# Sign transfers ahead of the q and k loads, the last pair's scaling in the gated block, and weight preparation over two pieces

## The chip, the cores and the metric

The kernel runs on one core of a Trainium2 chip, alone. The metric is the device time in microseconds of one execution of the whole program: the attention block, and the gated feed-forward block that takes its output. Five engines work side by side, each through its own list of instructions in order: TensorE (PE, with PEld for its weight loads), VectorE (DVE), ScalarE (ACT), GpSimd (POOL) and SyncE (SP). In this kernel POOL and SP do little but issue DMAs.

## What is computed

```python
# q, k, v: 4 batches x 8 heads x 768 x 64; proj: 64 x 6
q_bits = (np.einsum('bhsd,dk->bhsk', q, proj) > 0)
k_bits = (np.einsum('bhsd,dk->bhsk', k, proj) > 0)
# the buckets are the bits read as a number
mask = q_bucket[:, :, :, None] == k_bucket[:, :, None, :]
scores = np.where(mask, scale * np.matmul(q, k.transpose(0, 1, 3, 2)), -1e9)
attn = softmax(scores)
attn_out = np.matmul(attn, v)
# bridge: x is 3072 tokens x 512
g = x @ w_gate                      # 512 x 1536
silu = g * (1.0 / (1.0 + np.exp(-g)))
out = silu * (x @ w_val) @ w_out    # 1536 x 512
```

The three weight matrices are float64 and come to the chip as pairs of 32-bit words.

## The kernel before

**Attention** goes over 16 pairs of heads (4 batches of 4 pairs), each in two halves of 384 queries, each half in six chunks of 128 keys. For a chunk, PE multiplies q and k (`sc`, L427, with `T`), adds a product of bit rows (`qb`, `kb`) in the same PSUM bank, by which unequal buckets come out far below equal ones, ScalarE takes the exponential into one of eight tiles `A` (L430), and VectorE adds the tiles up into `acc` (L455, L459). After the six chunks PE multiplies them with v (`av`, L441).

The bits of pair n+1 are made in pair n's second half: PE's hash products, four sign instructions on ScalarE (L359), and for q a transfer on SP that copies the signs of 32 rows to a second place, `spread_q` (L371, qb<-qb). The first chunk of pair n+1 needs it. The q and k loads of pair n+2 (L245, and L253 from pair 5 on, eight DMAs of 96 KB) are issued on SP at the end of pair n's first half. Each has one buffer, so a load waits until pair n+1's transposes have read it: PE's transposes for the first pairs, VectorE's (L395) from pair 5 on.

The sums of pair n are made in pair n+1's first half: `total` (L464) with PE, a copy of a `row` on ScalarE (L473) and a small DMA few<-row on SP (L475). `invert` follows at the end of that half: VectorE's reciprocal (L479), then sums<-few and two r<-sums on SP (L481, L485). `norm` follows at the end of the second half: xT is scaled on VectorE (L491), and stored in DRAM (L496), or split into three parts for batch 0. For the last pair all three come after the loop (L545 to L548).

**Weight preparation** runs beside attention and the first part of the gated block. `prepare` (L131) is a generator: each piece of 128 x 512 weights takes five steps on VectorE (L140, L142, L145, L149, L151), with two scaling instructions on ScalarE ahead of them (L122, L123) and a rounding between the third and the fourth (L146). A step at the end writes the piece's three parts to DRAM from POOL (L153, ram<-stage), and later a ring tile loads them back (`bring`, L179, ring<-ram). There are 36 pieces. `prepare_on(n)` takes n steps: 4 or 5 at the end of each half in attention, one after each atom in the gated block. `scale_ahead` (L126) issues the two scaling instructions of a piece before its steps, in attention before and after the v products. Word tiles (`wordp`) have four buffers, staging tiles (`stagep`) two, ring tiles seven.

**The gated block** goes over 48 up blocks (4 batches of 12) and a down block for every three. An up block has four atoms: `one` and `other` for the gate and for the value. `one` is 16 matmuls into `a`, which ScalarE copies (L612); `other` is 8 matmuls into `n`, which VectorE subtracts (L618). The silu (L620), the product (L622), the hid copy (L623) and VectorE's two parts of it (L626, L628) follow. A down block has six atoms of nine matmuls (`o`), the first of a batch copied by ScalarE (L657). The PSUM tiles of this block are four, of two banks each, and go round: a gate's `a` and `n`, then a value's.

The order on each engine is that in which the program issues the instructions; no scheduler moves them.

Of the kernel before, what the change touches and what calls it, by code (L numbers as in the profile page):

```python
# [19 lines left out]
def kernel(  # L20
# [104 lines left out]

    def scale_ahead():  # L126
        i = progress["scaled"]
        if i < NPIECE and i < progress["kept"] + 2 and i in words:
            scale(i)

    def prepare():  # L131
        for i in range(NPIECE):
            load_words(i + 1)
            if i not in staged:
                scale(i)
            t, st = words[i], staged[i]
            lo, hi = t[:, :, 0], t[:, :, 1]
            w = st[:, 1]
            wi = w.bitcast(I32)
            nc.vector.tensor_single_scalar(wi, wi, 3, op=ALU.logical_shift_left)  # L140
            yield True
            nc.vector.scalar_tensor_tensor(out=wi, in0=hi, scalar=-(1 << 31), in1=wi,  # L142
                                           op0=ALU.bitwise_and, op1=ALU.bitwise_or)
            yield True
            nc.vector.tensor_tensor(wi, wi, lo, op=ALU.add)  # L145
            nc.scalar.activation(r32(st[:, 0]), w, AF.Copy, scale=TOWARD)  # L146
            load_words(i + 4)
            yield True
            nc.vector.tensor_tensor(r32(w), w, st[:, 0], op=ALU.subtract)  # L149
            yield True  # L150
            nc.vector.scalar_tensor_tensor(out=r32(st[:, 2]), in0=w, scalar=-STEP, in1=st[:, 0],  # L151
                                           op0=ALU.mult, op1=ALU.add)
            nc.gpsimd.dma_start(ram[i].bitcast(FP32), st)  # L153
            progress["kept"] = i + 1
            yield True
# [57 lines left out]
    def attention(scope):  # L213
# [116 lines left out]
        load_words(4)  # L330
# [79 lines left out]
        xT = {}  # L410
        mean = {}
# [21 lines left out]
        def attend(u):  # L433
# [30 lines left out]
        def total(n):  # L464
# [9 lines left out]
            few = att.tile([P, each], FP32, tag="few", name="few")  # L474
# [3 lines left out]
        def invert(n, few):  # L478
# [3 lines left out]
            t = att.tile([P, 2, HQ], FP32, tag="r", name="r")  # L482
# [72 lines left out]
    def gated_block(scope):  # L555
        xs = [even_x, scope.enter_context(tc.tile_pool(name="odd_x", bufs=1))]
# [121 lines left out]
        splits = []  # L678
        for kind, n in order:
            if kind == "U":  # L680
                b, f = divmod(n, NF)
                if f == NF - NQ and b + 1 < B:
                    for pr in range(NP):
# [3 lines left out]
                        splits += split(x, b + 1, pr, xs[(b + 1) % 2])  # L687
            if kind == "D" and n == B * NF // NQ - 1:
                finish(tails)
            for atom in atoms_of(kind, n):  # L690
# [4 lines left out]
                if splits:  # L695
                    splits.pop(0)()
                prepare_on(1)

    bring(7)
# [34 lines left out]
```

## Time and profile before

| | us |
|---|---|
| median of 8 runs | 1032.61 |
| lowest and highest | 1030.24, 1036.11 |
| the profiled execution | 1033.42 |
| its span, first to last instruction | 1031.6 |
| its mean granted PE clock | 0.965 |

Attention takes the first 418 us of the span, the gated block the rest. In the rows below, a time in front of an engine is the start from the beginning of the span, the next number is how long it took; in brackets stands for how long the engine had been idle before it, and what ended that. L numbers are lines of this kernel. In a row of a group, the numbers after the bar are the busy time in all, the mean of one in ns, and the idle time just before, with what ended it. PEclk is the clock that PE was granted, as a share of full speed. A row of a DMA with KB has the median from issue to landing as its last number.

### The profile page before, as it was taken

Reading aid. Unit: us, or ns where it says so; the run is one execution under the profiler, and the core shown is the slowest. Engines: PE = TensorE matmul, PEld = TensorE weight load, DVE = VectorE, ACT = ScalarE, POOL = GpSimd, SP = SyncE. Lnnn points to the kernel's source line nnn. Section 1 sums busy time; section 2 is a strip of 40 time slices with the busy share of each in tenths; the row PEclk is TensorE's granted clock in tenths of the full one; section 3 lists DMA queues with packets and bytes.
Section 4 is the critical chain, followed back from the end, with each engine's and each line's share of the span. In section 5 each row is a group of like instructions: output and inputs, shape, how many; then the busy total and the mean of one; then the engine's idle time right before and its main releaser. Section 6 shows DMA issues by size and latency. Waiting matters only on the chain.

```text
span 1031.6 us, 14465 instructions
## 1 busy us (share of the span) xinstructions
PE 964.8 (94%) x5413; PEld 728.4 (71%) x5413; DVE 674.3 (65%) x868; ACT 474.1 (46%) x882; POOL 125.2 (12%) x248
## 2 busy tenths in 40 slices
PE   8988888889788899599999999999999999999998
PEld 4444433334233344499999999999999999999997
DVE  5766776667567678287877654677554686555566
ACT  7877765666566668155342133232233133233221
POOL 3110000000001101132111111111101111111110
PEclk9989988889889899989999999999999999999999
DMA  7554555665656645797895575456656536746541
GB/s 200 165 156 146 134 139 128 181 181 131 181 131 181 181 130 182 276 334 265 337 341 195 192 299 198 179 174 216 247 209 245 184 135 249 259 151 217 197 171 62
DMA packets 134262, 203.22 MB, mean 197 GB/s; under 512 B 92912, under 2 KB 98512, under 8 KB 134192
## 3 DMA queue, kind: packets, MB, share of 16 engines
q0 software_dynamic: 31008, 159.79, 43.3%
q1 hardware_dynamic: 102384, 42.30, 16.2%
q8 instruction: 43, 0.70, 0.3%
q10 hardware_dynamic: 800, 0.20, 0.1%
q14 instruction: 27, 0.22, 0.1%
HBM read 162.01 MB, written 39.42 MB: 195 GB/s over the span
## 4 chain that ended last, share of the span: by engine, by line
PE 56%; DMA 2%; DVE 1%; issue 0%; SPq 0%; DVEq 0%
PE a L570 25%; PE o L570 18%; PE n L570 13%; DMA few<-row 1%; DVE o L662 0%; DVE o L659 0%; DMA r<-sums 0%; DMA sums<-few 0%; DVE g L618 0%; DVE stage L151 0%; SPq L485 0%; DVE few L479 0%; DVE xT L491 0%; DVEq L618 0%; DVEq L142 0%
## 5 line engine op out<-in xcount | busy, mean ns | idle before, releaser
L570 PE MATMUL a<-xparts,ring 128*128 128x384 f32 x1536 | 283.8, 336 | 1.9 <-ACT row L473 1.9
L570 PEld LDWEIGHTS a<-xparts,ring 128*128 128x128 f32 x1536 | 269.9, 189 | 3.8 <-ACT row L473 2.6
L570 PE MATMUL o<-ring,hid 128*128 128x512 f32 x864 | 199.1, 390 | 0.0
L427 PE MATMUL sc<-qT,kT 64*128 64x384 f32 x768 | 182.2, 539 | 13.2 <-ACT A L430 13.2
L570 PEld LDWEIGHTS o<-ring,hid 128*128 128x128 f32 x864 | 161.9, 188 | 33.1
L430 ACT ACTIVATE A<-sc 128x384 f32<-128x384 f32 x384 | 157.9, 501 | 42.6 <-PE sc L427 42.1
L427 PEld LDWEIGHTS sc<-qT,kT 64*128 64x128 f32 x768 | 79.0, 199 | 121.2 <-issue 87.6
L570 PE MATMUL n<-xparts,ring 128*128 128x384 f32 x768 | 149.9, 336 | 9.2 <-DVE g L618 9.2
L459 DVE TENSOR_TENSOR acc<-acc,A 128x768 f32<-128x768 f32 x128 | 122.7, 958 | 38.2 <-ACT A L430 27.2
L570 PEld LDWEIGHTS n<-xparts,ring 128*128 128x128 f32 x768 | 135.5, 189 | 9.5 <-DVE g L618 9.5
L441 PE MATMUL av<-A,vraw 128*64 128x386 f32 (+1 forms) x768 | 131.2, 491 | 0.0
L189 POOL DMA_DIRECT2D ring<-ram x144 | 76.1, 531 | 433.0 <-PE n L570 276.6
L618 DVE TENSOR_TENSOR v<-v,n 128x768 f32<-128x768 f32 x48 | 45.8, 954 | 105.9 <-PE n L570 104.8
L427 PE MATMUL sc<-qb,kb 64*128 64x384 bf16 x384 | 81.0, 342 | 35.5 <-DMA qb<-qb 34.9
L441 PEld LDWEIGHTS av<-A,vraw 128*64 128x64 f32 x768 | 52.3, 136 | 72.3 <-issue 60.0
L612 ACT ACTIVATE g<-a 128x768 f32<-128x768 f32 x48 | 39.0, 811 | 126.8 <-PE a L570 123.6
L623 ACT ACTIVATE hid<-v 128x768 fp32r<-128x768 f32 x48 | 40.7, 847 | 118.7 <-DVE v L622 118.7
L620 ACT ACTIVATE g<-g 128x768 f32<-128x768 f32 x48 | 40.6, 846 | 104.6 <-DVE g L618 104.6
L662 DVE TENSOR_TENSOR o<-o 128x512 f32<-128x512 f32 x96 | 65.9, 687 | 21.5 <-ACT o L657 19.0
L153 POOL DMA_DIRECT2D ram<-stage x36 | 19.7, 547 | 435.2 <-issue 228.6
L455 DVE SCALAR_TENSOR_TENSOR acc<-A 128x768 f32<-128x768 f32 x32 | 30.6, 957 | 63.5 <-ACT A L430 63.3
L618 DVE TENSOR_TENSOR g<-g,n 128x768 f32<-128x768 f32 x48 | 45.6, 950 | 30.1 <-PE n L570 30.1
(75 smaller groups left out, 732.0 us busy)
## 6 DMA issues: line engine op xcount, KB each, us to landing
ring<-ram POOLq DMA_DIRECT2D x144, 768.0 KB, 5.4
ram<-stage POOLq DMA_DIRECT2D x36, 768.0 KB, 4.9
vraw<-in_v_dram SPq DMA_DIRECT2D x16, 384.0 KB
r<-sums SPq DMA_DIRECT2D x32, 192.0 KB
words<-in_moe_w_out_dram POOLq DMA_DIRECT2D x12, 512.0 KB, 6.6
out_dram<-o SPq DMA_DIRECT2D x24, 256.0 KB
words<-in_moe_w_gate_dram POOLq DMA_DIRECT2D x11, 512.0 KB, 7.4
words<-in_moe_w_val_dram POOLq DMA_DIRECT2D x11, 512.0 KB, 7.8
```

What stands on the lines that cost most here:

```text
L189: nc.gpsimd.dma_start(t.bitcast(FP32), ram[at].bitcast(FP32))
L427: nc.tensor.matmul(sc[h], x["k", n][rows, ks], x["q", n][rows, qs], start=start, stop=not start)
L430: nc.scalar.activation(weights(u)[:, h, 0:HQ], sc[h], AF.Exp, scale=SCALE * (OFF / 2 if n <= NP else 1.0))
L441: nc.tensor.matmul(ps[h * D : (h + 1) * D, 0:width], raws["v", n][:, h, c, :], a[:, h, 0:width], start=c == 0, stop=c == NCH - 1)
L455: nc.vector.scalar_tensor_tensor(out=acc[n, half], in0=weights(u - 1)[:, :, 0:HQ], scalar=S * EPS / P, in1=a[:, :, 0:HQ], op0=ALU.add, op1 ...
L459: nc.vector.tensor_tensor(acc[n, half], acc[n, half], a[:, :, 0:HQ], op=ALU.add)
L570: nc.tensor.matmul(ps, w, x, start=start, stop=stop)
L612: nc.scalar.activation(two(z), ops[what][2], AF.Copy, scale=STEP + 1)
L618: nc.vector.tensor_tensor(two(z), two(z), n_, op=ALU.subtract)
L620: nc.scalar.activation(z, z, AF.Silu)
L623: nc.scalar.activation(h, val, AF.Copy, scale=TOWARD / STEP)
L662: nc.vector.tensor_tensor(accs[c], accs[c], t[:, 1], op=ALU.subtract)
```

## The change

There are three parts.

1. The q and k loads of pair n+2 are issued in the third chunk of pair n's second half, right behind the step that makes the signs and issues their spread, instead of at the end of the first half.
2. The last pair's `invert` and `norm` run in the gated block, after its 6th and 14th atom. Its xT and its spread reciprocals get a place in a tile of the gated block's x parts (`lastx`), so that attention's tiles can be given back. The first seven ring loads are issued one at the end of each of the last seven halves, instead of all seven behind the loop.
3. A piece's last two steps are taken after the next piece's first three, so that two pieces are under way. The rounding is no longer issued with the third step, but by the next `scale_ahead` (or at the latest ahead of the fourth step). `scale_ahead` may go three pieces beyond what is finished instead of two, and is also called after each atom of the gated block. Staging tiles get a third buffer, word tiles go from four buffers to three, and words are loaded three pieces ahead instead of four.

```diff
-    wordp = ctx.enter_context(tc.tile_pool(name="wordp", bufs=4))
-    stagep = ctx.enter_context(tc.tile_pool(name="stagep", bufs=2))
+    wordp = ctx.enter_context(tc.tile_pool(name="wordp", bufs=3))
+    stagep = ctx.enter_context(tc.tile_pool(name="stagep", bufs=3))
+    small = ctx.enter_context(tc.tile_pool(name="small", bufs=2))
+    odd_x = {NP - 1: ctx.enter_context(tc.tile_pool(name="odd_x", bufs=1))}
...
+    unrounded = []
+
+    def round_up():
+        st = staged[unrounded.pop(0)]
+        nc.scalar.activation(r32(st[:, 0]), st[:, 1], AF.Copy, scale=TOWARD)
+
     def scale_ahead():
+        if unrounded:
+            round_up()
         i = progress["scaled"]
-        if i < NPIECE and i < progress["kept"] + 2 and i in words:
+        if i < NPIECE and i < progress["kept"] + 3 and i in words:
             scale(i)
 
     def prepare():
...
+        for i in range(NPIECE + 1):
+            if i < NPIECE:
...
+                nc.vector.tensor_tensor(wi, wi, lo, op=ALU.add)
+                unrounded.append(i)
+                load_words(i + 3)
+                yield True
+            if i > 0:
+                while i - 1 in unrounded:
+                    round_up()
+                st = staged[i - 1]
+                w = st[:, 1]
+                nc.vector.tensor_tensor(r32(w), w, st[:, 0], op=ALU.subtract)
+                yield True
+                nc.vector.scalar_tensor_tensor(out=r32(st[:, 2]), in0=w, scalar=-STEP,
+                                               in1=st[:, 0], op0=ALU.mult, op1=ALU.add)
+                nc.gpsimd.dma_start(ram[i - 1].bitcast(FP32), st)
+                progress["kept"] = i
+                yield True
...
-                    xT[n] = xp.tile([P, S], FP32, tag="xT", name="xT")
-                    mean[n] = att.tile([P, 1], FP32, tag="e", name="e")
+                    if n == len(pairs) - 1:
+                        t = odd_x[NP - 1].tile([P, 3, S], FP32, tag=f"x{NP - 1}", name="lastx")
+                        xT[n], spread[n] = t[:, 0], t[:, 1]
+                    else:
+                        xT[n] = xp.tile([P, S], FP32, tag="xT", name="xT")
+                    mean[n] = small.tile([P, 1], FP32, tag="e", name="e")
...
                 if u + c == 2 or more and half == 1 and c == 2:
                     prepare_pair(1)
+                if half == 1 and c == 2:
+                    load(n + 2, "qk")
...
                 if n + 1 <= NP:
                     prepare_pair(2 if u else 4)
-                load(n + 2, "qk")
             prepare_on(5 if 0 < n < NP else 4)
+            if u >= N - 7 * NCH:
+                bring()
         total(len(pairs) - 1)
-        while waiting:
-            last.append(waiting.pop(0)())
-        finish(last)
+        left.extend(waiting)
...
+                    while next(preparing, None):
+                        pass
...
+                count[0] += 1
+                if left and count[0] in (6, 14):
+                    left.append(left.pop(0)())
+                    left[:] = [f for f in left if f]
                 prepare_on(1)
-
-    bring(7)
+                scale_ahead()
```

What moves stands in the orders of the engines. First SP, in a pair from which on each load of q or k is four DMAs; few, sums and r are the small transfers of the pair before, qb<-qb spreads the signs. Before (L253 loads q and k, L371 spreads):

```order
L475 DMA few<-row 128x1x12
L481 DMA sums<-few 128x12
L485 DMA r<-sums 64x768 x2
L253 DMA qraw<-in_q_dram 32x24x32 x4
L253 DMA kraw<-in_k_dram 32x24x32 x4
L371 DMA qb<-qb 32x768
L232 DMA vraw<-in_v_dram 128x2x384
```

And now (L268 loads, L386 spreads):

```order
L495 DMA few<-row 128x1x12
L501 DMA sums<-few 128x12
L508 DMA r<-sums 64x768 x2
L386 DMA qb<-qb 32x768
L268 DMA qraw<-in_q_dram 32x24x32 x4
L268 DMA kraw<-in_k_dram 32x24x32 x4
L247 DMA vraw<-in_v_dram 128x2x384
```

The eight loads have gone behind the spread; nothing else on SP has moved there.

Next ScalarE from the end of an early pair's second half (its signs of k are L359 before, L374 now) to the next pair's exponentials; L146 before and L132 now are the rounding, L122 and L123, now L124 and L125, the scaling. Before:

```order
L359 ACTIVATE kb<-hps,columns 32x384 x4
L200 ACTIVATE xparts<-xT 128x768
L122 ACTIVATE stage<-words 128x512
L123 ACTIVATE words<-words 128x512
L448 COPY xT<-av 128x384
L146 ACTIVATE stage<-stage 128x512
L430 ACTIVATE A<-sc 128x384 x4
```

And now:

```order
L374 ACTIVATE kb<-hps,columns 32x384 x4
L215 ACTIVATE xparts<-xT 128x768
L132 ACTIVATE stage<-stage 128x512
L124 ACTIVATE stage<-words 128x512
L125 ACTIVATE words<-words 128x512
L468 COPY xT<-av 128x384
L446 ACTIVATE A<-sc 128x384 x4
```

The rounding has gone from right ahead of the exponentials to ahead of the scaling, and it is that of the steps taken one half earlier.

Last ScalarE at the start of the gated block, now, with the buffers' numbers, from the first value's copy (L639) and hid (L650) to the second block's gate; L647 is the silu:

```order
L639 ACTIVATE v_3601<-a_3642 128x768
L650 ACTIVATE hid_3599<-v_3601 128x768
L124 ACTIVATE stage_3677<-words_3639 128x512
L125 ACTIVATE words_3639<-words_3639 128x512
L639 ACTIVATE g_3681<-a_3683 128x768
L647 ACTIVATE g_3681<-g_3681 128x768
```

And POOL at that place, where L168 writes a staging tile, L204 loads a ring tile and L117 loads words:

```order
L204 DMA ring_3670<-ram_88 128x1536
L168 DMA ram_106<-stage_3459 128x1536
L204 DMA ring_3713<-ram_89 128x1536
L117 DMA words_3742<-in_moe_w_val_dram 128x4x256
L204 DMA ring_3753<-ram_90 128x1536
L168 DMA ram_107<-stage_3542 128x1536
```

The staging tiles come in the order 3459, 3542, 3623, 3677, and there are three buffers: the tile that L124 writes here takes the buffer of 3459, which the second row of POOL's list writes out. Before, the scaling stood with the first step of its own piece, five steps after the write that it waits for. The gate copy of the second block (g_3681) stands behind the scaling.

More of the change, by code (lines that the diff above doesn't have):

```diff
@@ L410, in attention @@
         xT = {}
+        spread = {}
         mean = {}
@@ L473, in total @@
             nc.scalar.copy(row, ps[:, 0:HQ])
-            few = att.tile([P, each], FP32, tag="few", name="few")
+            few = small.tile([P, each], FP32, tag="few", name="few")
             nc.sync.dma_start(few, row.rearrange("(g r) t -> r g t", r=BLOCK)[0])
@@ L481, in invert @@
             nc.sync.dma_start(s, few)
-            t = att.tile([P, 2, HQ], FP32, tag="r", name="r")
+            if n == len(pairs) - 1:
+                t = spread[n].rearrange("p (x q) -> p x q", x=2)
+            else:
+                t = att.tile([P, 2, HQ], FP32, tag="r", name="r")
             flat = s.rearrange("p e -> (p e)").rearrange("(h x t) -> h (x t)", h=2, t=HQ)
@@ L555, in gated_block @@
     def gated_block(scope):
-        xs = [even_x, scope.enter_context(tc.tile_pool(name="odd_x", bufs=1))]
+        rest = scope.enter_context(tc.tile_pool(name="odd_x_rest", bufs=1))
+        xs = [dict.fromkeys(range(NP), even_x), {**dict.fromkeys(range(NP - 1), rest), **odd_x}]
         hidp = scope.enter_context(tc.tile_pool(name="hidp", bufs=4))
```

41 lines of the change are left out of this document (15 added, 26 removed).

## Prediction

> **What bounds the kernel now.** I read the page first, then PE's waits, then stretches cut at the same point of successive pairs, and last the hand-over from attention to the gated block.
>
> ```profile
> span 1031.6 us, 14465 instructions
> PE 964.8 (94%) x5413; PEld 728.4 (71%) x5413; DVE 674.3 (65%) x868; ACT 474.1 (46%) x882; POOL 125.2 (12%) x248
> PE   8988888889788899599999999999999999999998
> PEclk9989988889889899989999999999999999999999
> ```
>
> PE is the bound, and from the twentieth slice on (25.8 us a slice) it is full at full clock: nothing is to be won there. The slices before it have gaps, and a lower clock beside them. So the questions are who ends PE's waits in attention, and what the change puts into the part that is full.
>
> ```profile
> PE sc L427 <- DMA qb<-qb: 34.9, 10, 7.3
> PE sc L427 <- ACT A L430: 13.2, 7, 3.3
> ACT stage L146 <- DVE stage L145: 39.4, 20, 3.6
> ```
>
> These are waits between 40 and 411 us (total, times, longest). PE waits 34.9 us for the transfer that spreads the signs, and 13.2 us for exponentials that come late. The third row, ScalarE's, says why they are late: it stands at the rounding of a weight piece until VectorE has finished that piece's words, and the exponentials stand behind it.
>
> ```profile
> core 0: us, PE busy (x) PEld busy (x) DVE busy (x) ACT busy (x) POOL busy (x), PEclk, DMA share, GB/s
> 49.10:130.40 81.30, 71.62 (x434) 34.39 (x433) 56.60 (x74) 59.55 (x131) 7.08 (x12) 0.92 0.54 150
> 130.40:391.20 260.80, 222.77 (x1364) 97.70 (x1362) 180.81 (x243) 162.79 (x370) 19.47 (x32) 0.91 0.58 155
> 228.90:251.54 22.64, 21.31 (x138) 10.24 (x137) 17.36 (x24) 14.71 (x36) 1.06 (x2) 1.00 0.55 140
> 369.00:391.20 22.20, 20.87 (x139) 9.46 (x138) 17.89 (x26) 15.99 (x39) 2.11 (x4) 1.00 0.50 145
> 251.54:280.83 29.29, 22.03 (x137) 9.28 (x136) 18.21 (x26) 17.17 (x40) 2.34 (x4) 0.88 0.61 166
> ```
>
> The second stretch holds ten whole pairs: 26.1 us each. The third and fourth are single pairs in which PE did not wait for signs: PE is busy for 21.31 and 20.87 us at clock 1.00, and what is left is 1.33 us each. The last has the longest wait for signs: 29.29 us, at a clock of 0.88. So a pair costs about 21 us of PE at full clock, beside some 18 us of VectorE and 15 to 16 us of ScalarE.
>
> **The change, part by part.** *The q and k loads behind the spread.*
>
> ```profile
> 259.12 1.16 ACT L359 ACTIVATE qb<-hps,columns 32x384 bf16<-32x384 f32 x2
> 259.44 7.04 SPq L253 DMA_DIRECT2D qraw<-in_q_dram  x4
> 266.53 2.77 SPq L253 DMA_DIRECT2D kraw<-in_k_dram  x4
> 269.39 0.60 SPq L371 DMA_DIRECT2D qb<-qb  x1
> 273.96 0.47 PE L427 MATMUL sc<-qb,kb 64*128 64x384 bf16 x1 [7.26 <-DMA qb<-qb]
> 236.20 2.94 SPq L253 DMA_DIRECT2D qraw<-in_q_dram  x4
> 254.88 0.97 DVE L395 STREAM_TRANSPOSE kT<-kraw 128x768 f32<-128x768 f32 x1
> ```
>
> The signs are ready at 259.12 + 1.16 = 260.28. SP is then issuing the eight loads, until 269.3, and only then the spread; PE restarts at 273.96. After the change the spread goes at 260.3, and the 4.6 us that it took here end at 265, nine ahead of PE's need: the wait is gone. The loads start after it, about 1.5 us later than now. Queued behind them on SP are the x store, the v load, few<-row, sums<-few and r<-sums, later by as much; VectorE waits for the loads (its transposes) and for few (its reciprocal). Now the loads are issued at 236.20 and the transposes come at 254.88, 18.7 us later. At a pair of 21 us instead of 26, with the later issue, some 12 are left, while SP's issuing alone takes 6 to 10. That is close; VectorE has 20.87 - 17.89 = 3.0 us of slack a pair to cover it. I take nothing for it, and keep as the other end that the wait moves to VectorE (rival two).
>
> *Rounding one step behind, in attention.*
>
> ```profile
> 59.02 0.63 ACT L146 ACTIVATE stage<-stage 128x512 fp32r<-128x512 f32 x1 [3.60 <-DVE stage L145]
> ```
>
> Now the rounding is issued with the last addition to the words, ahead of the next half's exponentials. After the change it stands behind those twelve, and VectorE's share of them stands behind that last addition, so it is done by then. The 13.2 us go.
>
> The sum for attention: ten pairs at 21.31 (the pair that has its own q and k loads) instead of 260.80 gives 260.8 - 213.1 = 47.7; at 20.87 it would be 52.1. From 49.10 to 130.40 PE idles 81.30 - 71.62 = 9.7, and a clock of 0.92 is worth up to 0.08 x 81.3 = 6.5, of which I leave out 1.7 as lying in idle time: 14.5. The last pair has no more than half a microsecond to give: 0.5. Together **62.7**, with ends of 28 (rival two) and 68.
>
> *The last pair's reciprocal and scaling, and the first seven ring loads.*
>
> ```profile
> 417.90 3.05 PE L570 MATMUL a<-xparts,ring 128*128 128x384 f32 x16 [1.91 <-ACT row L473]
> 429.61 0.23 DVE L479 RECIPROCAL few<-few 128x12 f32<-128x12 f32 x1 [11.40 <-DMA few<-row]
> 435.90 1.02 DVE L491 SCALAR_TENSOR_TENSOR xT<-xT,e,r 128x768 f32<-128x768 f32 x1 [6.07 <-DMA r<-sums]
> 438.44 2.93 PE L570 MATMUL n<-xparts,ring 128*128 128x384 f32 x8 [9.18 <-DVE g L618]
> 637.59 2.77 PE a L570 x16
> 641.75 2.77 PE a L570 x16
> 463.74 12.28 PE o L570 x54
> ```
>
> VectorE stands 11.40 and 6.07 us for two small transfers of the last pair, with the gated block's first subtraction behind them, and PE stands 9.18 for that. At full speed 24 up-matmuls take 641.75 - 637.59 = 4.16 us, so the eight groups before the first down block take 33.3; here it starts 463.74 - 417.90 = 45.8 after the first. **12.6** us go: the two steps move to atoms 6 and 14, when their transfers are long over, and no ring load stands in a heap before them. Their 0.2 and 1.0 us of VectorE lie beside PE's matmuls. The ring loads go out one a half, beside q and k loads in two pairs only; the DMA share there is 0.50 to 0.61, so I take nothing.
>
> *The pipeline in the gated block.* Here the change adds a wait. After each atom, `scale_ahead` runs right behind `prepare_on(1)`. When a step ends a piece, it issues the write of a staging buffer, and in the same atom ScalarE is told to scale into a buffer that this write must leave first: the fourth staging tile takes the place of the first. Seven of the eight pieces scaled here stand so. Behind the scaling, on ScalarE, is the copy that empties the next gate's PSUM tile.
>
> ```profile
> L618 DVE TENSOR_TENSOR v<-v,n 128x768 f32<-128x768 f32 x48 | 45.8, 954 | 105.9 <-PE n L570 104.8 <-ACT v L612 0.8
> L622 DVE TENSOR_TENSOR v<-g,v 128x768 f32<-128x768 f32 x48 | 46.0, 957 | 1.7
> L151 DVE SCALAR_TENSOR_TENSOR stage<-stage 128x512 fp32r<-128x512 f32 x36 | 24.7, 685 | 0.8
> L612 ACT ACTIVATE g<-a 128x768 f32<-128x768 f32 x48 | 39.0, 811 | 126.8 <-PE a L570 123.6 <-issue 3.2
> L620 ACT ACTIVATE g<-g 128x768 f32<-128x768 f32 x48 | 40.6, 846 | 104.6 <-DVE g L618 104.6
> L623 ACT ACTIVATE hid<-v 128x768 fp32r<-128x768 f32 x48 | 40.7, 847 | 118.7 <-DVE v L622 118.7
> L620 ACT ACT_TABLE_LOAD x1 | 1.3, 1283 | 0.0
> L146 ACT ACTIVATE stage<-stage 128x512 fp32r<-128x512 f32 x36 | 22.6, 629 | 55.2 <-DVE stage L145 55.0
> L122 ACT ACTIVATE stage<-words 128x512 f32<-128x512 f32 x36 | 24.7, 686 | 3.6 <-DMA ram<-stage 3.2 <-ACT stage L146 0.4
> L123 ACT ACTIVATE words<-words 128x512 int32<-128x512 uint16 x36 | 24.6, 685 | 0.0
> ram<-stage POOLq DMA_DIRECT2D x10, 768.0 KB, 4.8
> words<-in_moe_w_out_dram POOLq DMA_DIRECT2D x3, 512.0 KB, 11.2
> ```
>
> The last two rows are of 418 to 540 us, the 4.8 and 11.2 from issue to landing. I walk the first hold, with 0 at PE's first gated matmul. ScalarE copies the gate from 2.8 to 3.6, rounds (0.6), scales (two steps, 1.3), loads its table (1.3), takes the silu (0.85), rounds again, and ends the copy of v at 9.1; the block's last n group ended at 8.3. VectorE's subtraction 0.95, product 0.96 and the piece's last step 0.69 end at 11.7; the write lands 4.8 later, at 16.5. ScalarE has had nothing since the hid copy at 11.8. Its two scaling steps end at 17.8, and the gate copy at 18.6. PE wants that tile (four of two banks go round) at 16.6, so it stands 2.0 us. The second hold starts from there: VectorE's chain ends at 26.6, the write lands at 31.4, the two steps, a silu and the v copy end at 34.3, and PE, at 31.1, stands 3.2. The third falls into the first down block, with the last pair's scaling in the chain, and costs 6.5; the fourth, with six copies and subtractions of that block behind it, 4.6; the others come to 3 to 4 each. Together **28** us, 4 a hold. The ends: 0, if the four tiles cover the holds, and 73, if the scaling waits 11.2 us (the slowest landing in that stretch, of words that it needs as well) instead of 4.8, 6.4 more for each of seven. The rounding gains nothing here, since it stands right behind VectorE's addition again. I take 28, because the chain of each hold is made of measured durations.
>
> A page bears on that size. The Trainium skill, "DMA: Bandwidth & Descriptors", section "Anatomy of one DMA — SWDGE (gpsimd) path", fits a transfer from this queue as 2.0 us plus its bytes over 436 GB/s: for 768 KB an estimate of 3.8 us. The row says 4.8, on a busy queue, and the row decides; by the page each hold would be 1.0 shorter and the sum 7 us lower, about 979.
>
> Sum: 1031.6 - 62.7 - 12.6 + 28 = 984.3 us of span. The profiled execution took 1033.42, 1.8 more than its span, and 0.8 more than the median of 1032.61; with the same 1.8 I predict **986**.
>
> **Rivals.** *One: the holds stay hidden.* ScalarE is busy a third of the gated block's time, and the tiles go round in two groups. For it speaks that the first hold is only 2 us longer than its cover; against it that each hold starts from the one before. Time: 986 - 28 = 958.
>
> *Two: the wait moves to VectorE.* The loads or few land late for the transposes or the reciprocal. The point is 3.0 us of slack a pair. Is VectorE held so long that the wait on PE stays at its mean of 34.9 / 10 = 3.5 us beyond the 21.31 of a pair, ten pairs cost 248 and save 13 instead of 47.7: 986 + 35 = 1021. For it speaks that SP's eight issues took 9.9 us; against it that they took 6 in the pair at 236.20 and that no wait of VectorE for loads shows now.
>
> *Three: slower.* One mechanism: the scaling in the gated block waits for landings on a queue that also carries ring loads and words. What attention and the hand-over save is 75.3; over seven holds that is 10.8 each, against 4.0 at a landing of 4.8. A microsecond of landing costs one a hold, so it decides at 11.6. At 13 us each hold costs 12.2: 1033.4 - 75.3 + 85 = 1043. For it speaks the row of 11.2; against it the 4.8 of the writes themselves.
>
> *Four: the change doesn't do what it says.* The order of SP and ScalarE shows both moves, so only chance against it is left; the time would be that of before.
>
> *Five: the holds cool PE's clock.* In attention the three waits of about 3.3 us before 130.40 left a clock of 0.92, 6.5 us over the stretch or 2.2 each, while the waits of 1.33 left 1.00. In the forecast six of the seven holds last 3 us or more; at 2.2 each they cost 13 more: 999. For it speaks that those waits are of the same length; against it that part of the lost clock lies in time in which PE would wait for ScalarE anyway. The Trainium skill, "TensorE: Matmul & The Clock Gate", section "Part 1: The HAM clock gate (the "warmup" mystery)", has the clock at half after an idle window of some 3.4 us, and the trace agrees for 7.26 (0.88) and 1.33 (1.00).
>
> **How the numbers follow.** The forecast has 0.47, rival one 0.15, two 0.13, three 0.05, four or a sum that cancels 0.04, five 0.16. The forecast's own range runs from 962 (attention at 68, holds at 10) to 1008 (holds at 50). The range given reaches from 952, just below rival one, to 1021, rival two. A measurement of this kernel tells about 0.2% from no change; by the cases, faster has 0.91, within 0.2% 0.03, slower 0.06.
>
> **What would show it.** Right: no wait of PE for qb, the clock at 1.00 through attention, pairs of 21 to 22 us, ScalarE no longer waiting for VectorE at the rounding there, the first gated matmul at about 355 us, no wait of VectorE for few; then, in the hundred microseconds after it, waits of ScalarE's scaling for ram<-stage, some 5 us each and seven times, and PE waiting for ScalarE's copies. Wrong: those waits there without gaps on PE (rival one), VectorE waiting for kraw or few in attention (rival two), or scaling that waits 10 us and more (rival three).

## The result, and the profile after

| | before | with the change |
|---|---|---|
| median, us | 1031.41 of 31 runs | 991.23 of 11 runs |
| lowest and highest | 1026.00, 1037.48 | 987.13, 994.94 |
| the profiled execution | 1033.42 | 993.74 |
| its span | 1031.6 | 991.9 |

The ratio is 0.9609, with a 95% interval from 0.9591 to 0.9627: 3.9% faster. The forecast was 986, and its range 952 to 1021. The lines of the page that answer to those of before (span, the engines' busy time, PE and its granted clock in 40 slices, now of 24.8 us each):

```profile
span 991.9 us, 14458 instructions
PE 950.0 (96%) x5413; PEld 722.4 (73%) x5413; DVE 672.5 (68%) x868; ACT 473.2 (48%) x882; POOL 124.9 (13%) x248
PE   9999989999999798778999999999999999999998
PEclk9999989999999899898999999999999999999999
```

Two things are to be seen. In the first fourteen slices, where before stood mostly 8, stands 9 but for the sixth and the fourteenth. And slices sixteen to nineteen (372 to 471 us) have 8, 7, 7 and 8 tenths: they lie in the gated block, which before was at 9 from its second slice on. The view of PE's waits, over the whole span, names both (engine, line, what it waited for; total, times, longest):

```profile
PE hps L369 <- DVE qT L410: 7.8, 2, 7.4
PE o L597 <- ACT v L639: 5.9, 1, 5.9
PE sc L443 <- DMA qb<-qb: 5.7, 3, 3.4
PE n L597 <- DVE o L689: 5.4, 1, 5.4
PE o L597 <- ACT g L639: 3.6, 1, 3.6
PE a L597 <- ACT g L639: 3.4, 1, 3.4
PE a L597 <- ACT v L639: 1.6, 2, 1.2
...
PE sc L443 <- ACT A L446: 0.2, 1, 0.2
```

Of 34.9 us of waiting for signs (qb) 5.7 are left, and of 13.2 for exponentials (A) 0.2. New are one wait of 7.4 us for a transpose (qT), in attention, and waits for ScalarE's copies (g, v) and what hangs on them (o) in the gated block. The gap of 9.18 behind the first subtraction is gone.

Stretches between the same points as before tell how much each place gave. The first two rows answer to 49.10:130.40 and 130.40:391.20, the third is a pair that nothing held up, then two halves of pairs in which PE waited (3.4 for qb, 7.4 for qT), then the first 109 us of the gated block:

```profile
core 0: us, PE busy (x) PEld busy (x) DVE busy (x) ACT busy (x) POOL busy (x), PEclk, DMA share, GB/s
49.10:113.70 64.60, 64.60 (x436) 31.27 (x434) 55.34 (x73) 59.45 (x132) 5.81 (x10) 1.00 0.63 175
113.70:336.10 222.40, 207.73 (x1362) 90.77 (x1360) 180.82 (x243) 162.70 (x370) 21.79 (x36) 0.97 0.80 200
235.80:255.90 20.10, 20.10 (x139) 8.82 (x137) 17.67 (x25) 16.38 (x38) 2.58 (x4) 1.00 0.80 210
135.30:152.20 16.90, 13.28 (x72) 5.43 (x70) 10.29 (x14) 8.56 (x19) 1.29 (x2) 0.80 1.00 230
317.20:336.10 18.90, 11.54 (x70) 4.76 (x68) 9.09 (x13) 8.61 (x22) 0.77 (x2) 0.82 0.80 232
360.73:470.00 109.27, 89.45 (x430) 82.24 (x431) 60.22 (x84) 38.78 (x58) 18.61 (x33) 0.91 0.65 234
```

The early stretch gained 81.30 - 64.60 = 16.7, the ten pairs 260.80 - 222.40 = 38.4, and the last pair 26.7 - 24.6 = 2.1 (before from 391.20 to 417.90, now from 336.10 to the first gated matmul at 360.73). That is 57.2 in attention, where the prediction had 62.7. Behind that matmul the gated part took 1031.6 - 417.9 = 613.7 before and takes 991.9 - 360.73 = 631.2 now: 17.5 longer. With the 12.6 of the hand-over gained, the holds cost 30.1. The last row says how: PE is idle for 109.27 - 89.45 = 19.8, and a clock of 0.91 is worth up to 0.09 x 109.27 = 9.8 more.

ScalarE's waits from 350 to 470 us hold the predicted sign:

```profile
ACT stage L124 <- DMA ram<-stage: 36.9, 7, 8.4
```

Seven waits of the scaling for the write of a staging buffer, 36.9 / 7 = 5.3 us each; "some 5 us each and seven times" was expected. The first, 1.95 us at 367.14, leaves no gap on PE; each of the other six is followed by one. The second, in the rows of the timeline of POOL, ScalarE and PE (start, duration, and in brackets the idle time and what ended it):

```profile
374.87 0.54 POOL L168 DMA_DIRECT2D ram<-stage  x1 [4.72 <-ACT hid L650]
...
379.12 0.66 ACT L124 ACTIVATE stage<-words 128x512 f32<-128x512 f32 x1 [4.51 <-DMA ram<-stage]
...
380.23 0.79 ACT L639 ACTIVATE g<-a 128x768 f32<-128x768 f32 x1
...
381.07 3.39 PE L597 MATMUL a<-xparts,ring 128*128 128x384 f32 x12 [3.42 <-ACT g L639]
```

The write is issued at 374.87; ScalarE, idle for 4.51 us, scales only at 379.12, 4.25 after the issue; the copy of the gate, which asks for nothing but PE's result, stands behind the two scaling steps and ends at 381.0, and PE stands 3.42 us for that copy's PSUM tile. (The estimate by the Trainium skill, "DMA: Bandwidth & Descriptors", section "Anatomy of one DMA — SWDGE (gpsimd) path", was 3.8 for such a write; 4.25 lies between it and the 4.8 taken from the profile of before.) Over all seven waits the time from the write's issue to the scaling is 3.7 to 5.8 us, 4.8 in the mean.

### The profile page after: what moved, and what is told of

The parts are those of the page before. It is cut to its first block, busy times and chain, and to the rows that moved or that the text cites. A ratio compares the mean times of both kernels' runs of the same rounds, so it can differ in the third digit from the quotient of the medians.

```text
span 991.9 us, 14458 instructions
## 1 busy us (share of the span) xinstructions
PE 950.0 (96%) x5413; PEld 722.4 (73%) x5413; DVE 672.5 (68%) x868; ACT 473.2 (48%) x882; POOL 124.9 (13%) x248
## 3 DMA queue, kind: packets, MB, share of 16 engines
q1 hardware_dynamic: 102384, 42.30, 17.8%
## 4 chain that ended last, share of the span: by engine, by line
PE 79%; DMA 7%; issue 6%; ACT 3%; SPq 2%; DVE 2%; ACTq 0%; DVEq 0%; POOLq 0%
PE a L597 23%; PE o L597 18%; PE sc L443 13%; PE n L597 11%; PE av L457 10%; DMA ram<-stage 4%; DMA qb<-qb 2%; SPq L268 2%; ACT A L446 1%; PE sum L490 1%; PE hps L369 1%; PE tps L356 1%; DVE o L689 1%; DMA xram<-xT 1%; ACT qb L374 1%
## 5 line engine op out<-in xcount | busy, mean ns | idle before, releaser
L597 PE MATMUL o<-ring,hid 128*128 128x512 f32 x864 | 204.6, 397 | 9.4 <-ACT v L639 5.9
L597 PEld LDWEIGHTS o<-ring,hid 128*128 128x128 f32 x864 | 165.4, 192 | 44.7 <-ACT v L639 6.3
L443 PE MATMUL sc<-qT,kT 64*128 64x384 f32 x768 | 166.6, 508 | 0.2 <-ACT A L446 0.2
L204 POOL DMA_DIRECT2D ring<-ram x144 | 75.9, 529 | 437.6 <-PE n L597 284.0
L443 PEld LDWEIGHTS sc<-qT,kT 64*128 64x128 f32 x768 | 69.7, 189 | 72.3 <-issue 54.6
L639 ACT ACTIVATE g<-a 128x768 f32<-128x768 f32 x48 | 38.9, 810 | 127.5 <-PE a L597 127.5
L650 ACT ACTIVATE hid<-v 128x768 fp32r<-128x768 f32 x48 | 40.7, 847 | 116.1 <-DVE v L649 116.1
L647 ACT ACTIVATE g<-g 128x768 f32<-128x768 f32 x48 | 40.6, 846 | 87.2 <-DVE g L645 87.2
L443 PE MATMUL sc<-qb,kb 64*128 64x384 bf16 x384 | 69.2, 325 | 7.2 <-DMA qb<-qb 5.7
L168 POOL DMA_DIRECT2D ram<-stage x36 | 19.7, 547 | 382.2 <-ACT A L446 212.4
L653 DVE SCALAR_TENSOR_TENSOR hid<-hid,v 128x768 fp32r<-128x768 f32 x48 | 45.9, 956 | 31.7 <-ACT hid L650 31.7
```

The costliest lines, as they stand in the source:

```text
L204: nc.gpsimd.dma_start(t.bitcast(FP32), ram[at].bitcast(FP32))
L443: nc.tensor.matmul(sc[h], x["k", n][rows, ks], x["q", n][rows, qs], start=start, stop=not start)
L597: nc.tensor.matmul(ps, w, x, start=start, stop=stop)
L639: nc.scalar.activation(two(z), ops[what][2], AF.Copy, scale=STEP + 1)
L647: nc.scalar.activation(z, z, AF.Silu)
L650: nc.scalar.activation(h, val, AF.Copy, scale=TOWARD / STEP)
```

## The experiments

Each ratio is to the kernel before, run beside the experiment on the same chip; 1033.58, 1032.78 and 1032.94 us were its medians beside the three groups. The intervals of the ratios reach 3 to 5 us to either side, so a difference of medians below some 5 us tells nothing by itself. Line numbers differ by a few between kernels.

### Is it the scaling that holds the gated block?

`scale_later` lets `scale_ahead` go only two pieces beyond what is finished in the gated block; in attention it stays at three.

```diff
-    def scale_ahead():
+    def scale_ahead(ahead=3):
...
-        if i < NPIECE and i < progress["kept"] + 3 and i in words:
+        if i < NPIECE and i < progress["kept"] + ahead and i in words:
...
                 prepare_on(1)
-                scale_ahead()
+                scale_ahead(2)
```

> The changed kernel, but in the gated block the scaling may go only two pieces beyond what is finished, so that the staging buffer it fills was written out a whole piece (five atoms) earlier. If the seven holds of ScalarE behind ram<-stage (36.9 us of waits between 350 and 470 us) cost PE its 19.8 us of gaps and the half clock beside them there, the waits for ram<-stage in the gated block fall below 3 us, PE has no gap of more than 1 us after its first gated matmul, and the time falls by 26 to 31 us, to 960 to 965. If those gaps come from the last pair's scaling or from the rounding behind VectorE, which both stay, the time falls by less than 10.

Measured: 963.90 us (959.57 to 970.43), ratio 0.9336 [0.9288, 0.9383]; against the changed kernel's 991.23 that is 27.3 less. ScalarE's waits from 350 to 470 us hold of the seven only this:

```profile
ACT stage L124 <- DMA ram<-stage: 1.4, 2, 1.0
```

And the window of the first 109 us from its first gated matmul at 361.50:

```profile
361.50:470.80 109.30, 109.30 (x594) 104.77 (x595) 85.54 (x118) 50.88 (x73) 25.20 (x45) 1.00 0.86 318
```

PE has no idle time and the full clock, and gets 594 matmuls done where it got 430 in the same time. With the holds both things went, the gaps and the clock: the spans differ by 991.9 - 962.9 = 29.0, which is the 19.8 + 9.8 = 29.6 read from the row above. The theory of the holds stands; the rival that they are hidden is out.

### What stands in attention: the ring loads beside the last pair's q and k

`ring_later` issues the seven ring loads two a half in the last four halves (2, 2, 2, 1).

```diff
-            if u >= N - 7 * NCH:
-                bring()
+            if u >= N - 4 * NCH:
+                bring(2 if u < N - NCH else 1)
```

> The changed kernel, but the first seven ring loads go out two a half in the last four halves of attention, when no q or k load is left, instead of one a half in the last seven. Theory: the 7.4 us gap of PE at 331 us is the last pair's k load, which SP needed 18 us to issue because ring loads stood on the same transfer engines; then VectorE's wait for kraw goes, and the time falls by 7.4 plus up to 3.4 of half clock: 980 to 984. Rival: the late load is the effect of the staging writes and word loads that are there anyway; then the gap stays and the time is 988 to 994. If two ring loads a half delay few or r, a new wait of VectorE for them shows in the last four halves.

Measured: 989.49 us (987.28 to 991.99), ratio 0.9580 [0.9543, 0.9616]. The interval overlaps that of the changed kernel, so the time alone tells nothing. The first gated matmul comes at 355.58 instead of 360.73, and the wait for the transpose is 4.15 instead of 7.36. That is a part of the expected effect, and the expected 980 to 984 was missed. The last four halves are not yet free of the loads: POOL issues the first two ring loads at 312.33, and SP is issuing the last pair's k loads from 310.04 to 314.33.

`both_later` has this edit and that of `scale_later`.

> Both edits together. If the two losses are independent, the gains add: 950 to 957. If the ring loads so late push the first staging writes of the gated block back, part of the first gain goes: 957 to 965.

Measured: 958.78 us (955.94 to 963.97), ratio 0.9287 [0.9248, 0.9325], a little above the expectation. Its first gated matmul is at 355.32, 6.2 us ahead of `scale_later`'s, and the span is 957.4, shorter by 5.5.

`ring_behind` undoes that part altogether: the seven loads stand in a heap behind the loop, as before.

```diff
-            if u >= N - 7 * NCH:
-                bring()
...
+    bring(7)
     with ExitStack() as scope:
         gated_block(scope)
```

> The changed kernel, but with the first seven ring loads issued in a heap behind the loop, as before. The last pair's reciprocal and scaling stay in the gated block. It measures what the ring loads cost inside attention. Theory (the loads of the last pair take SP 18 us to issue because of ring loads beside them, which holds VectorE's transpose for 8.8 us and PE for 7.4): the wait of VectorE for kraw is under 2 us and that of PE for hps under 2, attention ends 6 to 9 us sooner; the price is a wait of PE for the first ring tiles at the start of the gated block, 3 to 8 us, since the first tile then lands some 7 us after its issue. Sum: 985 to 993. Rival (the issuing takes 18 us for another reason, such as the word loads or the writes of pieces): waits for kraw and hps stay as they are and the time goes up by the wait for ring tiles, 994 to 1002.

Measured: 991.98 us (991.73 to 994.54), ratio 0.9612 [0.9572, 0.9651]: no difference in time, and yet the mechanism shows. First the changed kernel, the timeline of SP, POOL, VectorE and PE around the last pair's loads:

```profile
306.83 7.08 SPq L268 DMA_DIRECT2D qraw<-in_q_dram  x4
313.96 10.71 SPq L268 DMA_DIRECT2D kraw<-in_k_dram  x4
...
306.48 0.53 POOL L204 DMA_DIRECT2D ring<-ram  x1
...
316.39 0.53 POOL L204 DMA_DIRECT2D ring<-ram  x1
...
317.44 0.53 POOL L204 DMA_DIRECT2D ring<-ram  x1
...
329.43 0.98 DVE L410 STREAM_TRANSPOSE kT<-kraw 128x768 f32<-128x768 f32 x1 [8.78 <-DMA kraw<-in_k_dram]
...
331.33 0.85 PE L369 MATMUL hps<-qT,hash 128*32 128x384 f32 x2 [7.36 <-DVE qT L410]
```

SP spends 7.08 + 10.71 = 17.8 us on issuing eight loads, with three ring loads of 768 KB beside them; VectorE's transpose waits 8.78 for the last of them, and PE 7.36 for VectorE. Now `ring_behind`, the timeline of SP at the same loads:

```profile
303.79 6.99 SPq L268 DMA_DIRECT2D qraw<-in_q_dram  x4
310.81 4.59 SPq L268 DMA_DIRECT2D kraw<-in_k_dram  x4
```

And its waits of PE up to 440 us:

```profile
PE a L595 <- DMA ring<-ram: 9.4, 1, 9.4
...
PE hps L369 <- DVE qT L410: 1.1, 2, 0.6
```

Without ring loads the k loads take 4.59 instead of 10.71 to issue, and the wait for the transpose is 0.6 at most. What that gains PE gives back at once: it stands 9.4 us for the first ring tile. So spreading the ring loads is worth nothing in time where the change puts them. Another place was tried: `ring_last3` is `both_later` with the loads in the last three halves (3, 3, 1), behind the last pair's q and k.

```diff
-            if u >= N - 4 * NCH:
-                bring(2 if u < N - NCH else 1)
+            if u >= N - 3 * NCH:
+                bring(3 if u < N - NCH else 1)
```

> The version with the scaling in the gated block limited to two pieces, and the seven ring loads in the last three halves (three, three, one), so that none is issued before the last pair's q and k loads are through SP. Theory (each ring load beside those eight loads delays the transposes of the last pair): VectorE's wait for them falls from 4.1 us to under 1, PE's wait for qT from 2.0 to under 0.5, no wait for the first ring tile: 953 to 958 us. Rival (the ring loads in the last three halves now collide with few and r of pair 14 and with the first ring tiles' use): waits of 2 to 6 us for few or ring, 959 to 965 us.

Measured: 959.09 us (957.63 to 963.73), ratio 0.9290 [0.9265, 0.9316]. VectorE's waits from 130 to 350 us:

```profile
DVE few L499 <- DMA few<-row: 9.1, 5, 5.9
...
DVE kT L410 <- DMA kraw<-in_k_dram: 0.3, 1, 0.3
```

And PE's, over the whole span:

```profile
PE sum L490 <- DVE acc L479: 2.4, 1, 2.4
```

Both expectations came in part: the wait for the loads is gone, and a wait of 5.9 for few has come in its place; PE now stands 2.4 us for VectorE's sums. The first gated matmul is at 352.56, 2.8 earlier than in `both_later`; the medians, 958.78 and 959.09, can't be told apart. Nor are they clear of `scale_later`'s 963.90, since the intervals overlap: that a later place for the ring loads gains time shows in the traces, by 6 to 9 us at the first gated matmul (361.50 there), but not surely in the medians.

### The parts by themselves

`loads_only` is the kernel before with part 1 alone.

```diff
+                if half == 1 and c == 2:
+                    load(n + 2, "qk")
...
-                load(n + 2, "qk")
```

> The kernel before with the first part of the change alone: q and k loads issued behind the spread of the signs; rounding, buffers, the last pair's steps and the ring loads all as before. Theory (part one carries nearly all of what attention gained; parts two and three then give back about as much as they save, 14.5 and 12.6 against some 30 of holds): the waits of PE for qb go (34.9 us before), the waits for A behind the rounding (13.2) stay and grow a little, no holds in the gated block, the wait of VectorE for few of the last pair stays. Attention is shorter by 40 to 48 us, the gated part as before: 985 to 994 us, so within 0.5% of the changed kernel. Rival (without the rounding's delay taken out, the pace of pairs stays near 26, because ScalarE's standing at the rounding was the other half of the wait): 1005 or more, with waits of PE for A above 30 us.

Measured: 996.03 us (994.04 to 999.31), ratio 0.9646 [0.9610, 0.9683], so 36.8 us of gain from one moved call. PE's waits up to 440 us:

```profile
PE sc L427 <- ACT A L430: 22.3, 12, 3.3
...
PE sc L427 <- DMA qb<-qb: 2.1, 4, 0.9
```

And the windows of the ten pairs and of the early stretch:

```profile
130.40:357.50 227.10, 212.40 (x1362) 98.13 (x1360) 180.85 (x243) 159.60 (x370) 19.46 (x32) 0.98 0.67 179
...
49.10:130.40 81.30, 71.31 (x434) 34.59 (x432) 56.60 (x74) 59.72 (x131) 7.08 (x12) 0.92 0.52 150
```

The waits for signs go, as expected, and those for exponentials behind the rounding grow from 13.2 to 22.3: they are now the largest wait of the pairs. Ten pairs gain 260.8 - 227.1 = 33.7, the early stretch nothing. That is less than the 40 to 48 expected.

`round_at_once` is the changed kernel with the rounding issued with the third step again.

```diff
                 unrounded.append(i)
+                round_up()
                 load_words(i + 3)
```

> The changed kernel, but with the rounding issued with the third step again, ahead of the next half's exponentials; three staging buffers, the order of the steps and the scaling after each atom stay. Theory (the rounding's delay carries the 14.5 us of the early pairs): PE's waits for A in attention are 13 us or more again, and since pairs run faster they reach more of them: attention ends 12 to 22 us later, the gated block unchanged: 1003 to 1014 us. Rival (the waits for A came only together with those for signs, and go with them): under 3 us of waits for A, 990 to 994.

Measured: 1014.98 us (1012.81 to 1015.88), ratio 0.9824 [0.9790, 0.9858]: 23.8 more than the changed kernel, the theory's mechanism and a little more than its size. Waits of PE and of ScalarE up to 440 us:

```profile
PE sc L444 <- ACT A L447: 18.8, 13, 4.2
...
ACT stage L132 <- DVE stage L155: 53.9, 22, 9.0
```

ScalarE stands 22 times at the rounding, and PE 13 times for the exponentials behind it. Three staging buffers and the new order of the steps don't help as long as the rounding stands there.

`last_pair_in_attention` is the changed kernel with the last pair's two steps back at the end of attention.

```diff
         total(len(pairs) - 1)
-        left.extend(waiting)
+        while waiting:
+            last.append(waiting.pop(0)())
+        finish(last)
```

> The changed kernel, but with the last pair's reciprocal and scaling back at the end of attention; the first seven ring loads still go out one a half. It splits the second part of the change. Theory A (VectorE's waits of 11.4 and 6.1 us for few and r came from seven ring loads issued in a heap just ahead of them): with the loads spread, few and r land in 2 to 4 us each, the hand-over costs PE 0 to 4 us more than in the changed kernel: 991 to 996 us. Theory B (the wait comes from the place, whatever lies on the queues): few and r together still take 10 us or more and PE waits some 9 us for the first subtraction: 999 to 1004 us.

Measured: 1000.31 us (997.26 to 1004.27), ratio 0.9687 [0.9644, 0.9729]: 9.1 more than the changed kernel, which is theory B's time. The timeline of SP and VectorE:

```profile
364.48 0.33 SPq L501 DMA_DIRECT2D sums<-few  x1
370.58 1.10 SPq L508 DMA_DIRECT2D lastx<-sums  x2
...
364.22 0.23 DVE L499 RECIPROCAL few<-few 128x12 f32<-128x12 f32 x1 [1.11 <-DMA few<-row]
378.63 1.02 DVE L514 SCALAR_TENSOR_TENSOR lastx<-lastx,e 128x768 f32<-128x768 f32 x1 [14.18 <-DMA lastx<-sums]
```

And what PE waits for at the first subtraction, by the view of its waits:

```profile
PE n L599 <- DVE g L647: 7.5, 1, 7.5
```

Theory A was right for few alone: 1.11 us of waiting instead of 11.40. But the next two transfers, sums (from 364.48 until SP could go on at 370.58) and the spread of it, now take 14.18 together, beside ring loads that are issued in the gated block. The wait has only moved from one small transfer to the next; taking the steps away from that place is what helps. Whether the single ring loads hold these transfers there, no run tells.

`loads_first` is the changed kernel with part 1 undone.

```diff
-                if half == 1 and c == 2:
-                    load(n + 2, "qk")
...
+                load(n + 2, "qk")
             prepare_on(5 if 0 < n < NP else 4)
```

> The changed kernel with its first part undone: the q and k loads are issued at the end of the first half again, ahead of the spread. If the loads in front cost PE its waits for qb, those come back in pairs 5 to 14, 3 to 4 us each and 30 to 40 in total, with half clock beside them: 1025 to 1045. If the rounding was what made them long, and they shrink without it, the time rises by less than 20: below 1011.

Measured: 1052.08 us (1050.61 to 1055.29), ratio 1.0188 [1.0156, 1.0220], which missed the expectation on the slow side. PE's waits:

```profile
PE sc L443 <- DMA qb<-qb: 63.7, 12, 15.5
```

Parts 2 and 3 alone make the kernel slower, and two thirds of that lie behind attention: from the first gated matmul, at 425.27, on it takes 1053.4 - 425.27 = 628.1 us, 14.4 more than before, with seven waits of the scaling for ram<-stage in it (34.4 us). Attention is 7.4 us longer (425.27 against 417.90). PE no longer waits for exponentials there, but its waits for signs grow from 34.9 to 63.7, and the longest, 15.5, falls into the halves in which ring loads go out as well. The growth, 28.8, is more than the 13.2 that the exponentials had cost, so that PE comes earlier to signs that are no earlier can explain only a part of it; the rest was not tested. Part 1 is worth 36.8 by itself and 60.9 on top of the others.

`split_loads` is `both_later` with the k loads issued half a pair earlier, so that only four loads stand behind the spread.

```diff
-                    load(n + 2, "qk")
+                    load(n + 2, "q" if n + 1 > NP else "qk")
...
+            if half == 0 and n + 1 > NP:
+                load(n + 2, "k")
```

> The version with the scaling in the gated block limited to two pieces and the ring loads two a half in the last four halves, and in addition the k loads of a pair are issued half a pair earlier (at the end of the first half, ahead of the small transfers), only the q loads behind the spread. Theory (what is left of PE's waits in attention, 2.0 us for qT, 2.2 for kb and 2.4 for qb, comes from eight loads in one row on SP): the wait for qT goes, SP's row behind the spread is half as long, 952 to 957 us. Rival (the four k loads ahead of the spread and of the small transfers delay these as before the change, since there they stand behind other transfers): waits for qb or few come back, 960 to 975 us.

Measured: 969.35 us (967.55 to 974.29), ratio 0.9389 [0.9363, 0.9414]; the rival was right. PE's waits:

```profile
PE sc L443 <- DMA qb<-qb: 16.6, 9, 4.6
```

And VectorE's from 130 to 350 us:

```profile
DVE xT L514 <- DMA r<-sums: 24.8, 8, 4.9
```

Four loads ahead of the small transfers delay these (r, eight times) and the spread behind them (qb, nine times). What the change gained it gained by that order, and half of the loads ahead of the spread bring back 10.6 us of time (969.35 against 958.78).

## Why the prediction was right, and where it was not

**Who ends PE's waits in attention: right.** Signs and exponentials were named as the two causes, and removing either cause removed its wait (5.7 and 0.2 left). The first gated matmul was to come at about 355 us and came at 360.73.

**The sum for attention, 62.7, was too high by 5.5, and its largest term, the 47.7 of the ten pairs, was wrongly sized** (the early stretch, counted as 14.5, gave 16.7). A pair was to cost 21.31; a pair that nothing holds costs 20.10, so the ten could have gained 260.8 - 201.0 = 59.8 instead of 47.7. They gained 38.4, because 222.4 - 201.0 = 21.4 were lost again: by their row, 14.7 of idle time and up to 6.7 by a clock of 0.97. Most of it lies in the two held stretches in the table, which lose 16.9 - 10.1 = 6.8 and 18.9 - 10.1 = 8.8 against half of 20.10. So 12.1 us that were not counted on came in and 21.4 that were not expected went out; that the sum is near in spite of this is luck. The step that failed is "the DMA share there is 0.50 to 0.61, so I take nothing". That share belonged to pairs of 26 us in the mean. About the same bytes in pairs of 22.7 us made it 0.67 (`loads_only`); in the changed kernel, at 22.2 us and with ring loads added, it is 0.80. At the ring loads the issuing of SP's eight loads took 17.8 us, not the "6 to 10" of before. What came was rival two's mechanism, VectorE late by loads, at one pair instead of ten. That ring loads cause it is shown: they go, and it goes (`ring_behind`).

"No wait of PE for qb" failed in the other held half, and twice by less. The changed kernel's rows of that half:

```profile
135.51 1.16 SPq L508 DMA_DIRECT2D r<-sums  x2
136.76 0.58 SPq L386 DMA_DIRECT2D qb<-qb  x1
...
144.15 0.48 PE L443 MATMUL sc<-qb,kb 64*128 64x384 bf16 x1 [3.42 <-DMA qb<-qb]
```

ScalarE's two sign instructions (L374) start at 132.79 and take 1.16, so the signs are ready at 133.95, but SP issues their spread only at 136.76. Ahead of it in SP's order stands r<-sums, for which SP waits 3.1 us until sums<-few has landed. And from the spread's issue to PE's restart it is 7.4 us, and 7.3 and 7.8 at the two shorter waits, where the prediction took 4.6. So the spread can still be late behind the small transfers, and its landing was sized too short. Why it lands so late, with the eight loads right behind it, a DMA share of 1.00 and no ring loads under way, no run tells.

**How attention's gain divides was wrong too.** The loads alone brought 33.7 in the ten pairs, not 47.7, and the rounding's move is worth 23.8 where 14.5 were counted, all of it before 130 us. The waits behind the rounding were taken as the early pairs' matter. Before, 9.5 of their 13.2 us lay there; with the loads alone it is 10.0 of 22.3, and the 12.3 in the later pairs show where they have grown.

**The hand-over, 12.6: near.** Putting the two steps back cost 9.1. The heap of ring loads was not the whole cause: with those spread, the wait went from few to the next transfers.

**The holds, 28: right in place, and in sum by luck.** They cost 27.3 by `scale_later`, and 30.1 by the spans. Seven waits of 5.3 us were there. The landing taken for them, 4.8, is the mean that came. The walk's first hold is the wait shown above, 4.51 of ScalarE's idle time where the walk gave 16.5 - 11.8 = 4.7; the 1.95 before it was not in the walk. The parts of the sum were different: PE's own gaps come to 19.8 in six places, not 28 in seven, two of them being small (1.6 us together), and the other 9.8 are the clock, which the forecast left out and rival five had put at 13. The two errors cancel.

**Rivals.** One (holds hidden) is out by `scale_later`. Three (slower) needed landings of 11.6 us; the seven were 3.7 to 5.8. Four is out. Five's mechanism was there, together with shorter gaps than it assumed.

By the runs, the parts are worth 36.8 (loads), 23.8 (rounding), 9.1 (last pair's place), nothing (ring loads) and -27.3 (holds): 42.4, against 40.2 measured. The loads' part is measured here on the kernel before and the others on the changed one. With the 60.9 that the loads are worth in the changed kernel the sum would be 66.5, so the parts depend on each other, and the agreement is no proof of the split. Without the holds the same change is worth 6.6% (0.9336), with the ring loads moved as well 7.1% (0.9287, `both_later`); these two intervals overlap.

## What to carry to other kernels

An engine that works ahead must not wait in order for a buffer that the last step has only just begun to write out: the wait of 5 us stands in front of every copy behind it, and "one piece further ahead" with as many buffers as pieces is such a wait each time. Before a transfer is taken as free, its neighbours' share is to be worked out at the pace after the change, for the faster kernel moves the same bytes in less time. And two waits in one loop are not priced one by one: here the loads' move was worth 37 us alone and 61 on top of the other parts, and the waits behind the rounding grew when those for the signs had gone.

## What was not expected of the hardware

A short wait can cost nearly twice its length. In the changed kernel's 3.42 us wait for signs at 140.7 a stretch at half clock began, here the row of a window laid around it:

```profile
143.15:149.98 6.83, 5.83 (x23) 2.38 (x24) 4.18 (x6) 2.23 (x5) 1.29 (x2) 0.50 0.93 179
```

PE's 5.83 us of work there would be 2.9 at full clock, so with the clock the wait cost 2.9 us more than its own 3.42. The length of the wait alone doesn't decide. In `split_loads`, one half has a wait of 2.1 us for signs, and another one of 2.3 (idle time 13.90 - 11.78 and 12.70 - 10.38):

```profile
163.10:177.00 13.90, 11.78 (x70) 4.87 (x68) 8.80 (x13) 9.02 (x20) 0.00 (x0) 0.88 0.78 176
...
187.10:199.80 12.70, 10.38 (x71) 4.47 (x69) 8.55 (x13) 9.00 (x20) 1.29 (x2) 1.00 0.74 206
```

The shorter one cost clock, the longer one none. The Trainium skill, "TensorE: Matmul & The Clock Gate", section "Part 1: The HAM clock gate (the "warmup" mystery)", has the clock fall after an idle window of some 3.4 us, in windows that run freely. A wait of 2.1 us at which the clock came down disagrees with it as to the length; that windows of its own, not the wait's start, decide would fit that one such wait does and another does not, but no run here was made to tell.

The other is SP's issuing. The four k loads of a pair took 2.77 us to issue in a row of before, 4.59 in `ring_behind`, and 10.71 beside ring loads in the changed kernel. So an engine that does nothing but issue can be the one that is late, and in the views it shows only as long rows of SP, not as a wait.
